# Second mixture of a three-stage kernel: work placed on the other side of skipped branches, and a 512-column product

## The chip, the cores and the metric

One core of a Trainium2 chip. The metric is device time in microseconds (us) of one execution of the whole kernel; smaller is better. A profile of one execution shows what each engine did: PE (TensorE; PEld is its weight load), DVE (VectorE), ACT (ScalarE), POOL (GpSimd) and SP (SyncE, which here only issues DMAs). Each engine has its own instruction stream and its own sequencer; they wait for one another with semaphores.

## The reference

Three stages, each fed by the one before. Only the last one matters for the change.

```python
attn = _attn_ref(x, a, B, C)              # linear attention, 4 x 8 heads x 768 steps
x = attn.transpose(0, 2, 1, 3).reshape(3072, 256)
x = _moe_ref(x, ...)                      # first mixture: 4 experts, every token through each
# second mixture: 8 experts, each token goes to one of them
expert_idx = argmax(x @ w_gate); gate_w = softmax(x @ w_gate)[expert_idx]
disp[e, k] = x[i]                         # k-th token of expert e, at most capacity = 768 of them
h = maximum(disp @ w1[e], 0)              # 256 -> 1024
y = h @ w2[e]                             # 1024 -> 256
out[i] = gate_w[i] * y[expert_idx[i], k]
```

## The kernel before

Every f32 operand of a product is split into a high and a low part (`h`, `l`), and a product is three matmuls: high by high, high by low, low by high.

The attention and the first mixture are one long stream without branches. The second mixture takes the experts 0 to 7 in turn. The tokens of an expert lie in a DRAM table `disp`; they are loaded in a block of up to 384 rows (`SLOTS`), transposed on PE (`turn`, L695) and split on ACT and DVE (`turned`, L703 and L704). How many tokens an expert has is known only when the kernel runs, so each expert has several programs, chosen by branches on the count: a narrow one for up to 256 tokens (`NARROW`), a wide one for up to 384, and a full one that does a wide block and then a second block of 384.

A block (`expert_block`, L737) loops over the 8 slices f of 128 hidden units. `up_part` (L715) makes a slice with six matmuls (L725 to L727) into a PSUM tile; ACT writes its high part after the ReLU (`ring_hh`, L729), DVE the low part (`ring_hl`, L730). Two slices later (`LAG` = 2) the slice is used for the second layer: for each group of 128 tokens, three matmuls of 256 columns, `hh` by `w2h`, `hh` by `w2l`, `hl` by `w2h` (L763 to L765), add into `yy`. At the block's end ACT scales each `yy` by the gate (`yo`, L773) and POOL scatters it to `out` by an indirect DMA (L774).

Between experts: `head(e)` (L732) does the first 256 columns of the first three slices (`HEAD`) of expert e before the count of e is asked, 18 matmuls in all; a wide or full program later adds the columns 256 to 384 of those three slices. Then come two branches in a row (L1090 and L1093): the narrow program, entered if the count is at most 256, and the wide or full ones, entered if it is more. Inside the latter, L1095 and L1097 choose between wide and full. Every branch runs on every engine. A program that isn't entered is jumped over, and on the other side stands, for each engine, an instruction that raises its semaphore by what the skipped program would have raised it (EVENT_SEMAPHORE in the trace), so that all later waits can count in program order. `hint` (L781) announces a later jump to PE's sequencer, and `align` (L784) sets the address of the next PE instruction to a slot of a block of 256 instructions. While an expert runs, its program also loads and splits the weights of the expert two further on (`split_w`, L365: a cast on ACT, a subtraction on DVE or POOL), and loads and turns the rows of the next one. The last expert has its own nesting of branches without jumps on its wide or full path.

Expert 0 is special: its first block is computed before the routing of the last tokens is done, on the rows known so far; `numbers["known"]` is their count. If that is below 384, the block has to be done once more; this is `redo_first` (L1061), asked at the very end (L1063).

Of the kernel before, what the change touches and what calls it, by code (L numbers as in the profile page):

```python
# [8 lines left out]
F32 = mybir.dt.float32  # L9
F32R = mybir.dt.float32r  # L10
# [21 lines left out]
SLOTS = 384  # L32
NARROW = 256
HEAD = 3
JOIN = 8
BLOCKS = [2, 3, 4, 4, 4, 4, 3]
MOST = max(BLOCKS)
NMAX = MOST * P
# [30 lines left out]
def attention_moe_moe_kernel(ctx: ExitStack, tc: tile.TileContext, aps: dict, cap: int):  # L69
# [282 lines left out]
    def weight_src(moe, e, c):  # L352
        w1, w2 = aps[f"w1_{moe}"][e], aps[f"w2_{moe}"][e]
        if c < 2:
            return w1[P * c:P * c + P, :]
        return w2[512 * (c - 2):512 * (c - 2) + 512, :].rearrange("(f p) d -> p f d", p=P)

    def load_w(moe, e, c):
        if (moe, e, c) not in given:
            pool, n = (late_pool[0], 2) if moe == 2 and (4 * e + c) % 5 > 2 else (sp, 3)  # L360
            given[moe, e, c] = pool.tile([P, FF], F32, tag="stage", name=f"stg{moe}_{e}_{c}", bufs=n)
        st = given[moe, e, c]
        nc.sync.dma_start(st if c < 2 else st.rearrange("p (f d) -> p f d", d=DM), weight_src(moe, e, c))

    def split_w(moe, e, c, lo):  # L365
        if (moe, e) not in W:
            W[moe, e] = [wp.tile([P, KD * FF], F32R, tag=n, name=f"{n}_{moe}_{e}") for n in ("w1h", "w1l", "w2h", "w2l")]
# [363 lines left out]

    def head(e):  # L732

        for f in range(HEAD):
            up_part(e, 0, f, 0, NARROW, f == HEAD - 1)

    def expert_block(e, k, n, extra, have=0, last=None, own=True):  # L737
        w2h, w2l = W[2, e][2:]
        g = gi[e, k]
        y = []  # L740
        at_ = 0

        def go():
            nonlocal at_
            at_ += 1
            for p in extra.get(at_, []):
                p()

        for f in range(NF + LAG):
            if f < NF:  # L750
                a = NARROW if f < have else 0
                if a < n:
                    up_part(e, k, f, a, n)
                go()
            js = [f - LAG] if LAG <= f < NF else list(range(NF - LAG, NF)) if f == NF else []
            for st in range(n // P):
                if js and js[0] == 0:
                    y.append(ps.tile([P, DM], F32, tag="acc", name=f"yy{e}_{k}_{st}", bufs=3))
                q = slice(P * st, P * st + P)
                for j in js:  # L760
                    hh, hl = ring[j % len(ring)]
                    c = slice(DM * j, DM * j + DM)
                    nc.tensor.matmul(y[st], lhsT=hh[:, q], rhs=w2h[:, c], start=j == 0, stop=False)  # L763
                    nc.tensor.matmul(y[st], lhsT=hh[:, q], rhs=w2l[:, c], start=False, stop=False)  # L764
                    nc.tensor.matmul(y[st], lhsT=hl[:, q], rhs=w2h[:, c], start=False, stop=j == NF - 1)  # L765
                if last and f == NF:
                    for p in last.get(st, []):
                        p()
            if js:
                go()  # L770
        for st in range(n // P):
            o = gp.tile([P, ROW], F32, tag="row", name=f"yo{e}_{k}_{st}", bufs=MOST)[:, :DM]
            nc.scalar.activation(o, y[st], AF.Copy, scale=g[:, st, 0:1])  # L773
            i = nc.gpsimd.indirect_dma_start(  # L774
                out=out[:, :],
                out_offset=bass.IndirectOffsetOnAxis(ap=g.bitcast(I32)[:, st, 1:2], axis=0),
                in_=o[:, :], in_offset=None, bounds_check=TOK - 1, oob_is_err=False)
            if own:
                disjoint("out", i)
# [7 lines left out]

    new_xT(0)
    steps0 = [attention_pieces(i, *xT[0], P * i) for i in range(2)]
    spare = wp.tile([P, 2 * FF], F32, tag="w2l", name="spare0")  # L790
    given[0, "bcq"] = given[1, "bcq"] = spare[:, 0:FF]
    given[1, "lt"] = spare[:, FF:].rearrange("p (h i) -> p h i", i=P)
    spare = wp.tile([P, 2 * FF], F32, tag="w2h", name="spare1")
# [9 lines left out]
    for tag, users in (("w1h", ((0, 2),)), ("w1l", ((1, 0), (3, 0))), ("w2h", ((1, 2), (3, 2))), ("w2l", ((2, 0),))):  # L803
        spare = wp.tile([P, 2 * FF], F32, tag=tag, name=f"early_{tag}")
        for e, c in users:
            given[1, e, c], given[1, e, c + 1] = spare[:, 0:FF], spare[:, FF:]

# [195 lines left out]
    W[2, 3] = [wp.tile([P, KD * FF], F32R, tag=n, name=f"{n}_2_3") for n in ("w1h", "w1l", "w2h", "w2l")]  # L1003
    for e in range(4, E2):
        W[2, e] = W[2, e - 4]
    for i in range(5, len(order)):
# [7 lines left out]

    make_ring()

    def first_block(e, n, two=False, over=None):
# [20 lines left out]
        expert_block(e, 0, n, extra, HEAD)  # L1038

    def second_into(e, tokens):  # L1040
        expert_block(e, 1, SLOTS, {})
        for k in range(2, nblk):
            with tc.If(tokens > SLOTS * k):
# [2 lines left out]
                turned(e, k)  # L1046
                expert_block(e, k, SLOTS, {})

    between = final_routing()
    between[10] = [load_counts]  # L1050
    first, second = ahead[0], ahead[1:]
    expert_block(0, 0, SLOTS, between, last={
        0: [lambda: ready(*first)], ST - 1: [lambda b=b: ready(*b) for b in second]})
    counts = numbers["all"]
    tokens = counts[0]
    if nblk > 1:
        with tc.If(tokens > SLOTS, preferred_fallthrough_block=True):
            second_into(0, tokens)
            align(JOIN)

    def redo_first():  # L1061

        with tc.If(numbers["known"] < SLOTS, preferred_fallthrough_block=True):  # L1063
            W[2, 0] = W[2, E2 - 1]
            for c in range(4):
                given[2, 0, c] = given[2, E2 - 1, c]
                load_w(2, 0, c)
                split_w(2, 0, c, nc.vector)
            load_rows(0, 0)
            ready(0, 0)  # L1070
            expert_block(0, 0, SLOTS, {}, own=False)

    for e in range(1, E2):
        tokens = counts[e]
        head(e)
        if e == E2 - 1:
            with tc.If(tokens > NARROW, preferred_fallthrough_block=True) as wide:
                if nblk > 1:
                    with tc.If(tokens > SLOTS, preferred_fallthrough_block=True) as more:
                        first_block(e, SLOTS, two=True)  # L1080
                        second_into(e, tokens)
                    with more.Else():
                        first_block(e, SLOTS)
                else:
                    first_block(e, SLOTS)
            with wide.Else():
                first_block(e, NARROW)
            redo_first()
            continue
        with tc.If(tokens <= NARROW, label=f"wide{e}", preferred_fallthrough_block=True):  # L1090
            hint(f"over{e}")
            first_block(e, NARROW)
        with tc.If(tokens > NARROW, label=f"over{e}", preferred_fallthrough_block=True):  # L1093
            if nblk > 1:
                with tc.If(tokens <= SLOTS, label=f"full{e}", preferred_fallthrough_block=True):  # L1095
                    first_block(e, SLOTS, over=f"next{e}")
                with tc.If(tokens > SLOTS, label=f"next{e}", preferred_fallthrough_block=True):  # L1097
                    first_block(e, SLOTS, two=True)
                    second_into(e, tokens)
                    align(JOIN)  # L1100
            else:
                first_block(e, SLOTS)


def prepare(inputs):
# [51 lines left out]
```

## Time and profile before

| | us |
|---|---|
| median of 3 runs (lowest, highest) | 791.07 (789.83, 792.62) |
| the profiled execution | 795.09 |
| its span, first to last instruction | 793.3 |
| busy PE / DVE / ACT / POOL | 766.5 / 440.8 / 282.9 / 189.0 |
| mean granted TensorE clock | 0.991 |

The span is what the trace's clock runs over; 1.8 us lie around it. A busy share counts the time in which an engine has an instruction in work; matmuls overlap, so on PE the distance between two starts (the pitch) says more than a duration.

In this data the trace shows expert 0 with a first and a second block (607.6 to 645.8 us), the experts 1 and 3 wide, 2, 4, 5 and 6 narrow, and 7 full (748.9 to 785.4 us). The count `known` is at least 384.

### The profile page before, as it was taken

The numbers are of one execution on the slowest core, as the hardware profiler recorded it, in microseconds if no ns is written. First come the engines' busy times: TensorE is split into PE (matmuls) and PEld (weight loads), VectorE is DVE, ScalarE is ACT, GpSimd is POOL, SyncE is SP. The second block draws the span as 40 slices with busy tenths as digits, with TensorE's granted clock in tenths as the row PEclk, the third lists the DMA queues.
The fourth block names the chain that finished last, engine by engine and source line by source line (L and its number), as shares of the span: only waits on it lengthen the run. The fifth ranks groups of instructions, "written<-read, shape, count | busy, mean of one in ns | idle before, by whom it ended". The sixth has DMA issues, their size and how long they took to land. (4 is left out here: it accounts for less than half of the span.)

```text
span 793.3 us, 13459 instructions
## 1 busy us (share of the span) xinstructions
PE 766.5 (97%) x5114; PEld 685.7 (86%) x5114; DVE 440.8 (56%) x884; ACT 282.9 (36%) x555; POOL 189.0 (24%) x227
## 2 busy tenths in 40 slices
PE   8999999999999999999999999999999989998996
PEld 7889999988878888888888888889999989897995
DVE  5886778457754577645666456543444323546321
ACT  2542543232323332233332323322453334555331
POOL 1010102212111122110221103011765313654211
PEclk9999999999999999999999999999999999999999
DMA  9753567523220232201322112040353214453100
GB/s 261 246 174 104 183 213 226 165 84 103 80 83 14 71 110 83 83 14 67 111 84 83 46 52 96 14 143 12 117 163 107 75 44 144 141 169 109 43 21 23
DMA packets 50195, 82.54 MB, mean 104 GB/s; under 512 B 5104, under 2 KB 35009, under 8 KB 50108
## 3 DMA queue, kind: packets, MB, share of 16 engines
q1 hardware_dynamic: 46340, 74.50, 30.0%
q0 software_dynamic: 2400, 6.11, 2.1%
q10 hardware_dynamic: 1368, 0.81, 0.4%
q8 instruction: 50, 0.82, 0.4%
q14 instruction: 37, 0.30, 0.1%
HBM read 65.56 MB, written 16.31 MB: 103 GB/s over the span
## 5 line engine op out<-in xcount | busy, mean ns | idle before, releaser
L502 DVE SCALAR_TENSOR_TENSOR hl<-ph,hh 128x512 fp32r<-128x512 f32 (+2 forms) x216 | 133.9, 620 | 221.7 <-ACT hh L501 218.1
L501 ACT ACTIVATE hh<-ph 128x512 fp32r<-128x512 f32 (+2 forms) x216 | 117.4, 543 | 348.4 <-PE ph L498 337.6
L496 PE MATMUL ph<-xh,w1h 128*128 128x512 f32 (+2 forms) x432 | 160.7, 372 | 1.6 <-DVE hl L502 1.6
L525 PE MATMUL acc<-hh,w2h 128*128 128x512 f32 (+2 forms) x432 | 158.1, 366 | 2.3 <-DVE x L541 1.4
L497 PE MATMUL ph<-xl,w1h 128*128 128x512 f32 (+2 forms) x432 | 156.4, 362 | 0.0
L498 PE MATMUL ph<-xh,w1l 128*128 128x512 f32 (+2 forms) x432 | 156.4, 362 | 0.0
L526 PE MATMUL acc<-hl,w2h 128*128 128x512 f32 (+2 forms) x432 | 156.3, 362 | 0.0
L527 PE MATMUL acc<-hh,w2l 128*128 128x512 f32 (+2 forms) x432 | 156.1, 361 | 0.0
L525 PEld LDWEIGHTS acc<-hh,w2h 128*128 128x128 f32 x432 | 81.2, 188 | 13.9 <-DVE x L541 2.2
L496 PEld LDWEIGHTS ph<-xh,w1h 128*128 128x128 f32 x432 | 81.3, 188 | 12.5 <-DVE hl L502 2.3
L730 DVE SCALAR_TENSOR_TENSOR ring_hl<-qh,ring_hh 128x384 fp32r<-128x384 f32 (+2 forms) x82 | 38.5, 472 | 95.8 <-ACT ring_hh L729 88.3
L498 PEld LDWEIGHTS ph<-xh,w1l 128*128 128x128 f32 x432 | 81.2, 188 | 10.5
L527 PEld LDWEIGHTS acc<-hh,w2l 128*128 128x128 f32 x432 | 81.3, 188 | 10.4
L526 PEld LDWEIGHTS acc<-hl,w2h 128*128 128x128 f32 x432 | 81.3, 188 | 9.4
L497 PEld LDWEIGHTS ph<-xl,w1h 128*128 128x128 f32 x432 | 81.3, 188 | 8.7
L549 POOL TENSOR_TENSOR x<-x,cmb 128x512 f32<-128x512 f32 (+2 forms) x40 | 48.5, 1234 | 153.0 <-DVE cmb L546 152.9
L729 ACT ACTIVATE ring_hh<-qh 128x384 fp32r<-128x384 f32 (+2 forms) x82 | 34.9, 425 | 83.8 <-PE qh L727 81.0
L765 PE MATMUL yy<-w2h,ring_hl 128*128 128x256 f32 x208 | 59.8, 287 | 0.0
L763 PE MATMUL yy<-w2h,ring_hh 128*128 128x256 f32 x208 | 59.7, 287 | 0.0
L764 PE MATMUL yy<-w2l,ring_hh 128*128 128x256 f32 x208 | 59.7, 287 | 0.0
L180 DVE TENSOR_TENSOR_SCAN lt<-abc,id 128x512 f32<-128x512 f32 x44 | 57.4, 1304 | 0.0
L725 PE MATMUL qh<-sxh,w1h 128*128 128x256 f32 (+2 forms) x132 | 42.0, 318 | 10.8 <-DVE ring_hl L730 3.0
(166 smaller groups left out, 1080.8 us busy)
## 6 DMA issues: line engine op xcount, KB each, us to landing
stg<-in_w SPq DMA_DIRECT2D x34, 512.0 KB
abc<-a_zero SPq DMA_DIRECT2D x21, 512.0 KB
bcr<-in_bc SPq DMA_DIRECT2D x19, 512.0 KB
disp<-zrow SPq DMA_DIRECT2D x12, 516.0 KB
nat<-in_nat SPq DMA_DIRECT2D x24, 256.0 KB
pb<-pT SPq DMA_DIRECT2D x16, 256.0 KB
rw<-disp SPq DMA_DIRECT2D x10, 387.0 KB
out<-zrow SPq DMA_DIRECT2D x6, 512.0 KB
```

Of the source, the lines that this page charges most:

```text
L180: nc.vector.tensor_tensor_scan(t["lt"][:, sl, :].rearrange("p h i -> p (h i)"), a_bc[:, sl, :].rearrange("p h i -> p (h i)"), id4.rearrang ...
L496: nc.tensor.matmul(ph[:, :n], lhsT=wh[:, c], rhs=xh[:, k, :n], start=k == 0, stop=False)
L497: nc.tensor.matmul(ph[:, :n], lhsT=wh[:, c], rhs=xl[:, k, :n], start=False, stop=False)
L498: nc.tensor.matmul(ph[:, :n], lhsT=wl[:, c], rhs=xh[:, k, :n], start=False, stop=k == KD - 1)
L501: nc.scalar.activation(hh[:, :n], ph[:, :n], AF.Relu)
L502: nc.vector.scalar_tensor_tensor(hl[:, :n], ph[:, :n], 0.0, hh[:, :n].bitcast(F32), ALU.max, ALU.subtract)
L525: nc.tensor.matmul(a[:, :n], lhsT=wh[:, c], rhs=hh[:, :n], start=f == 0, stop=False)
L526: nc.tensor.matmul(a[:, :n], lhsT=wh[:, c], rhs=hl[:, :n], start=False, stop=False)
L527: nc.tensor.matmul(a[:, :n], lhsT=wl[:, c], rhs=hh[:, :n], start=False, stop=f == NF - 1)
L763: nc.tensor.matmul(y[st], lhsT=hh[:, q], rhs=w2h[:, c], start=j == 0, stop=False)
L764: nc.tensor.matmul(y[st], lhsT=hh[:, q], rhs=w2l[:, c], start=False, stop=False)
L765: nc.tensor.matmul(y[st], lhsT=hl[:, q], rhs=w2h[:, c], start=False, stop=j == NF - 1)
```

## The change

The two halves of a second-layer weight become one tile `[128, 2, 2048]`, and the products of `hh` with both halves one matmul of 512 columns into a PSUM tile `[128, 2, 256]`; `hl` by `w2h` adds to its first half. At the block's end ACT scales the first half as before, and a new DVE instruction adds the second half times the gate. The three PSUM tiles are allocated once and used in rotation.

`head(e + 1)` no longer stands between the branches of two experts. It stands three times: in the Else of the branch that skips all wide programs, in the Else of the one that skips the full program, and at the end of the full program. In the Else of the narrow program stands `first_down`: the second-layer products of the first two slices for 256 tokens, which the wide and full programs then leave out. The repeat of expert 0's first block is asked right after expert 0, with `head(1)` in its Else. The last expert gets the same branches as the others. `JOIN` goes from slot 8 to 0, and expert 0's first block is aligned to slot 190 after its first slice.

```diff
-JOIN = 8
+JOIN = 0
+FIRST_BLOCK = 190
...
+    def weights(moe, e):
+        w1 = [wp.tile([P, KD * FF], F32R, tag=n, name=f"{n}_{moe}_{e}") for n in ("w1h", "w1l")]
+        w2 = wp.tile([P, 2, KD * FF], F32R, tag="w2", name=f"w2_{moe}_{e}")
+        return [*w1, w2[:, 0], w2[:, 1], w2]
...
+    def down_part(e, y, q, j):
+        w2 = W[2, e][4]
+        hh, hl = ring[j % len(ring)]
+        c = slice(DM * j, DM * j + DM)
+        nc.tensor.matmul(y, lhsT=hh[:, q], rhs=w2[:, :, c], start=j == 0, stop=False)
+        nc.tensor.matmul(y[:, 0], lhsT=hl[:, q], rhs=w2[:, 0, c], start=False, stop=j == NF - 1)
...
+    def sums(e, k, st):
...
+        return totals[(2 * e + k + st) % 3]
+
+    def first_down(e, y):
+
+        for j in range(LAG):
+            for st, t in enumerate(y):
+                down_part(e, t, slice(P * st, P * st + P), j)
...
-                    nc.tensor.matmul(y[st], lhsT=hh[:, q], rhs=w2h[:, c], start=j == 0, stop=False)
-                    nc.tensor.matmul(y[st], lhsT=hh[:, q], rhs=w2l[:, c], start=False, stop=False)
-                    nc.tensor.matmul(y[st], lhsT=hl[:, q], rhs=w2h[:, c], start=False, stop=j == NF - 1)
+                    if st >= len(early[1]) or j >= lead:
+                        down_part(e, y[st], q, j)
...
-            nc.scalar.activation(o, y[st], AF.Copy, scale=g[:, st, 0:1])
+            nc.scalar.activation(o, y[st][:, 0], AF.Copy, scale=g[:, st, 0:1])
+            nc.vector.scalar_tensor_tensor(o, y[st][:, 1], g[:, st, 0:1], o, ALU.mult, ALU.add)
...
+    def choose(cond, label, yes, no):
+        with tc.If(cond, label=label, preferred_fallthrough_block=True) as choice:
+            yes()
+        if no:
+            with choice.Else():
+                no()
+
+    def full_program(e, tokens, y):
+        first_block(e, SLOTS, y, LAG, two=True)
+        second_into(e, tokens)
+        head(e + 1)
+        if e + 1 < E2:
+            align(JOIN)
+
+    def wide_programs(e, tokens, y, after):
...
+        choose(tokens <= SLOTS, f"full{e}", lambda: first_block(e, SLOTS, y, LAG, over=f"next{e}"), None)
+        choose(tokens > SLOTS, f"next{e}", lambda: full_program(e, tokens, y), after)
+
+    def narrow_program(e, y):
+        hint(f"over{e}")
+        first_block(e, NARROW, y, 0)
+
+    def first_once_more():
+        load_rows(0, 0)
+        ready(0, 0)
+        expert_block(0, 0, SLOTS, {}, own=False)
+        head(1)
+        align(JOIN)
+
     between = final_routing()
+    between[1] = [lambda: align(FIRST_BLOCK)]
...
-        with tc.If(tokens > SLOTS, preferred_fallthrough_block=True):
-            second_into(0, tokens)
-            align(JOIN)
+        with tc.If(counts[0] > SLOTS, preferred_fallthrough_block=True):
+            hint("again")
+            second_into(0, counts[0])
+    choose(numbers["known"] < SLOTS, "again", first_once_more, lambda: head(1))
     for e in range(1, E2):
         tokens = counts[e]
-        head(e)
...
+        after = (lambda: head(e + 1)) if e + 1 < E2 else None
+        y = [sums(e, 0, st) for st in range(NARROW // P)]
+        choose(tokens <= NARROW, f"wide{e}", lambda: narrow_program(e, y), lambda: first_down(e, y))
+        choose(tokens > NARROW, f"over{e}", lambda: wide_programs(e, tokens, y, after), after)
```

## Rows read from the trace of the kernel before

**Rows 1.** The page: busy time of each engine, and PE's granted clock in 40 slices.
```profile
PE 766.5 (97%) x5114; PEld 685.7 (86%) x5114; DVE 440.8 (56%) x884; ACT 282.9 (36%) x555; POOL 189.0 (24%) x227
PEclk9999999999999999999999999999999999999999
```
**Rows 2.** Two windows: us, busy PE, PEld, DVE, ACT, POOL, granted clock, DMA, GB/s.
```profile
652.90:656.40 3.50, 3.50 (x16) 3.50 (x16) 0.29 (x1) 1.21 (x2) 1.98 (x1) 0.52 0.00 0
717.80:721.30 3.50, 3.19 (x16) 2.89 (x14) 0.42 (x1) 0.89 (x3) 0.75 (x1) 0.51 0.42 143
```
**Rows 3.** Timeline of PE, starts of heads: start, us, instruction, idle before and releaser.
```profile
669.89 0.38 PE L725 MATMUL qh<-sxh,w1h 128*128 128x256 f32 x1 [0.75 <-ACTq L1097]
...
682.40 0.28 PE L765 MATMUL yy<-w2h,ring_hl 128*128 128x256 f32 x1
683.37 0.38 PE L725 MATMUL qh<-sxh,w1h 128*128 128x256 f32 x1 [0.69 <-ACTq L1093]
...
748.86 0.39 PE L725 MATMUL qh<-sxh,w1h 128*128 128x256 f32 x1 [0.68 <-ACTq L1093]
```
**Rows 4.** Line L1093's branch around 682 us: min/median/max ns, first and last start.
```profile
L1093 PEldq COMPARE_BRANCH  x1: 343/343/343, 681.7 to 681.7; - x1
...
L1093 PEldq EVENT_SEMAPHORE  x1: 51/51/51, 682.7 to 682.7; - x1
...
L1093 ACTq EVENT_SEMAPHORE  x1: 17/17/17, 683.3 to 683.3; - x1
```
**Rows 5.** Timeline of PE: after expert 0, and after a skipped narrow program.
```profile
645.55 0.28 PE L765 MATMUL yy<-w2h,ring_hl 128*128 128x256 f32 x1
647.25 0.36 PE L725 MATMUL qh<-sxh,w1h 128*128 128x256 f32 x1 [1.42 <-ACT yo L773]
...
649.36 0.28 PE L727 MATMUL qs<-sxh,w1l 128*128 128x256 f32 x1
650.63 0.33 PE L725 MATMUL qh<-sxh,w1h 128*128 128x128 f32 x1 [0.99 <-DVEq L1090]
```
**Rows 6.** Timeline of PE: ends of a 256-column run (27 matmuls) and a 512-column run (66).
```profile
764.59 0.28 PE L763 MATMUL yy<-w2h,ring_hh 128*128 128x256 f32 x1
...
767.70 0.28 PE L765 MATMUL yy<-w2h,ring_hl 128*128 128x256 f32 x1
...
471.42 0.50 PE L496 MATMUL ph<-xh,w1h 128*128 128x512 f32 x1
...
486.29 0.39 PE L498 MATMUL ph<-xh,w1l 128*128 128x512 f32 x1
```
**Rows 7.** Groups of instructions by shape: line, count, busy us, mean ns, idle before.
```profile
L763 PE MATMUL yy<-w2h,ring_hh 128*128 128x256 f32 x208 | 59.7, 287 | 0.0
L773 ACT ACTIVATE yo<-yy,gi 128x256 f32<-128x256 f32 x26 | 12.2, 477 | 15.4 <-PE yy L765 15.4
L730 DVE SCALAR_TENSOR_TENSOR ring_hl<-qh,ring_hh 128x256 fp32r<-128x256 f32 x34 | 14.2, 422 | 40.2 <-ACT ring_hh L729 34.6 <-issue 5.5
```
**Rows 8.** Timelines inside narrow expert 4: PE's two waits, and DVE before the second.
```profile
712.92 0.39 PE L725 MATMUL qh<-sxh,w1h 128*128 128x256 f32 x1 [0.39 <-DVE ring_hl L730]
...
716.54 0.39 PE L725 MATMUL qh<-sxh,w1h 128*128 128x256 f32 x1 [1.93 <-DVE ring_hl L730]
...
712.79 3.36 DVE L372 TENSOR_TENSOR w2l<-stg,w2h 128x1024 fp32r<-128x1024 f32 x1
```
**Rows 9.** Line L1090's branch around 650 us, columns as in rows 4.
```profile
L1090 DVEq COMPARE_BRANCH  x1: 69/69/69, 650.1 to 650.1; - x1
L1090 DVEq EVENT_SEMAPHORE  x1: 21/21/21, 650.6 to 650.6; - x1
```
**Rows 10.** Branch rows of lines L1090 and L1063, whole run.
```profile
L1090 PEldq COMPARE_BRANCH  x10: 72/190/232, 647.4 to 747.0; - x10
...
L1063 PEldq COMPARE_BRANCH  x1: 3018/3018/3018, 783.9 to 783.9; - x1
...
L1063 POOLq INC_SWDGE_SEM  x1: 530/530/530, 790.4 to 790.4; - x1
```

More of the change, by code (lines that the diff above doesn't have):

```diff
@@ L363, in load_w @@
         nc.sync.dma_start(st if c < 2 else st.rearrange("p (f d) -> p f d", d=DM), weight_src(moe, e, c))
+    def weights(moe, e):
+        w1 = [wp.tile([P, KD * FF], F32R, tag=n, name=f"{n}_{moe}_{e}") for n in ("w1h", "w1l")]
+        w2 = wp.tile([P, 2, KD * FF], F32R, tag="w2", name=f"w2_{moe}_{e}")
+        return [*w1, w2[:, 0], w2[:, 1], w2]
     def split_w(moe, e, c, lo):
         if (moe, e) not in W:
-            W[moe, e] = [wp.tile([P, KD * FF], F32R, tag=n, name=f"{n}_{moe}_{e}") for n in ("w1h", "w1l", "w2h", "w2l")]
+            W[moe, e] = weights(moe, e)
         h, l = W[moe, e][2 * (c // 2):2 * (c // 2) + 2]
@@ L732, in head, with expert_block @@
     def head(e):
-        for f in range(HEAD):
+        for f in range(HEAD if e < E2 else 0):
             up_part(e, 0, f, 0, NARROW, f == HEAD - 1)
-    def expert_block(e, k, n, extra, have=0, last=None, own=True):
-        w2h, w2l = W[2, e][2:]
+    def down_part(e, y, q, j):
[4 more added lines that the diff above has]
+        nc.tensor.matmul(y[:, 0], lhsT=hl[:, q], rhs=w2[:, 0, c], start=False, stop=j == NF - 1)
+    totals = []
+    def sums(e, k, st):
+        if not totals:
+            totals.extend(ps.tile([P, 2, DM], F32, tag="acc", name=f"yy{i}", bufs=3) for i in range(3))
+        return totals[(2 * e + k + st) % 3]
[3 more added lines that the diff above has]
+                down_part(e, t, slice(P * st, P * st + P), j)
+    def expert_block(e, k, n, extra, have=0, last=None, own=True, early=(0, ())):
         g = gi[e, k]
-        y = []
+        lead, y = early[0], list(early[1])
         at_ = 0
@@ L756, in expert_block @@
             for st in range(n // P):
-                if js and js[0] == 0:
-                    y.append(ps.tile([P, DM], F32, tag="acc", name=f"yy{e}_{k}_{st}", bufs=3))
+                if js and st == len(y):
+                    y.append(sums(e, k, st))
                 q = slice(P * st, P * st + P)
                 for j in js:
-                    hh, hl = ring[j % len(ring)]
-                    c = slice(DM * j, DM * j + DM)
-                    nc.tensor.matmul(y[st], lhsT=hh[:, q], rhs=w2h[:, c], start=j == 0, stop=False)
-                    nc.tensor.matmul(y[st], lhsT=hh[:, q], rhs=w2l[:, c], start=False, stop=False)
-                    nc.tensor.matmul(y[st], lhsT=hl[:, q], rhs=w2h[:, c], start=False, stop=j == NF - 1)
+                    if st >= len(early[1]) or j >= lead:
+                        down_part(e, y[st], q, j)
                 if last and f == NF:
@@ L789, in attention_moe_moe_kernel @@
     steps0 = [attention_pieces(i, *xT[0], P * i) for i in range(2)]
-    spare = wp.tile([P, 2 * FF], F32, tag="w2l", name="spare0")
+    both = wp.tile([P, 2, 2 * FF], F32, tag="w2", name="spare0")
+    spare = both[:, 1]
     given[0, "bcq"] = given[1, "bcq"] = spare[:, 0:FF]
     given[1, "lt"] = spare[:, FF:].rearrange("p (h i) -> p h i", i=P)
-    spare = wp.tile([P, 2 * FF], F32, tag="w2h", name="spare1")
+    spare = both[:, 0]
     given[1, "m0"] = spare[:, 0:512].rearrange("p (h i) -> p h i", i=P)
@@ L802, in attention_moe_moe_kernel @@
     given[1, 2, 2], given[1, 2, 3] = spare[:, 0:FF], spare[:, FF:]
-    for tag, users in (("w1h", ((0, 2),)), ("w1l", ((1, 0), (3, 0))), ("w2h", ((1, 2), (3, 2))), ("w2l", ((2, 0),))):
-        spare = wp.tile([P, 2 * FF], F32, tag=tag, name=f"early_{tag}")
+    both = wp.tile([P, 2, 2 * FF], F32, tag="w2", name="early_w2")
+    for spare, users in (
+            (wp.tile([P, 2 * FF], F32, tag="w1h", name="early_w1h"), ((0, 2),)),
+            (wp.tile([P, 2 * FF], F32, tag="w1l", name="early_w1l"), ((1, 0), (3, 0))),
+            (both[:, 0], ((1, 2), (3, 2))), (both[:, 1], ((2, 0),))):
         for e, c in users:
@@ L1000, in load_counts @@
         numbers["all"] = nc.values_load_multi_w_load_instructions(cnt[1][0:1, 0:E2], min_val=0, max_val=TOK)[1]
-    W[2, 3] = [wp.tile([P, KD * FF], F32R, tag=n, name=f"{n}_2_3") for n in ("w1h", "w1l", "w2h", "w2l")]
+    W[2, 3] = weights(2, 3)
     for e in range(4, E2):
@@ L1015, in attention_moe_moe_kernel, with first_block @@
     make_ring()
-    def first_block(e, n, two=False, over=None):
+    def first_block(e, n, y, lead, two=False, over=None):
         extra = {}
@@ L1037, in first_block @@
                 add(m + 3, lambda w=order[i + 5]: load_w(2, *w))
[L1038 removed]
+        expert_block(e, 0, n, extra, HEAD, early=(lead, y))
     def second_into(e, tokens):
@@ L1047, in second_into @@
                 expert_block(e, k, SLOTS, {})
+    def choose(cond, label, yes, no):
[11 more added lines that the diff above has]
+    def wide_programs(e, tokens, y, after):
+        if nblk == 1:
+            first_block(e, SLOTS, y, LAG)
+            head(e + 1)
+            return
+        choose(tokens <= SLOTS, f"full{e}", lambda: first_block(e, SLOTS, y, LAG, over=f"next{e}"), None)
[9 more added lines that the diff above has]
+        align(JOIN)
     between = final_routing()
+    between[1] = [lambda: align(FIRST_BLOCK)]
     between[10] = [load_counts]
@@ L1054, in attention_moe_moe_kernel @@
     counts = numbers["all"]
-    tokens = counts[0]
     if nblk > 1:
-        with tc.If(tokens > SLOTS, preferred_fallthrough_block=True):
-            second_into(0, tokens)
-            align(JOIN)
[L1061 to L1071, printed above, removed]
+        with tc.If(counts[0] > SLOTS, preferred_fallthrough_block=True):
+            hint("again")
+            second_into(0, counts[0])
@@ L1073, in attention_moe_moe_kernel @@
+    choose(numbers["known"] < SLOTS, "again", first_once_more, lambda: head(1))
     for e in range(1, E2):
         tokens = counts[e]
-        head(e)
[L1076 to L1102, printed above, removed]
+        after = (lambda: head(e + 1)) if e + 1 < E2 else None
```

## The prediction

> **What bounds the kernel now.** The page comes first: PE is in work for 97% of the span, no other engine for more than 56% [rows 1]. So time is won only where PE has less to do, waits less, or runs at a higher clock. [...] Then the timeline of PE, read for starts: within the second mixture PE pauses almost only between programs. Before each head but the first it has idled 0.68 to 0.75 us, six times, and the releaser is a branch instruction of ACT [rows 3]. The branch's own rows tell why: PE has jumped at 681.7 + 0.34 us, its own count is raised at 682.7, when its last matmul is through, but ACT, still scaling the block, reaches its raising instruction only at 683.3 [rows 4]; the head starts 0.07 us later. After a skipped narrow program PE has idled 0.99 us for DVE in the same way, and after expert 0 it has idled 1.42 us [rows 5].
>
> **The change part by part.** All sums are made against the profiled execution, 795.09 us (span 793.3 and 1.8 around it), and the difference is then taken from the median, 791.07.
>
> *The 512-column product.* A run of 27 matmuls of 256 columns has 26 pitches in 767.70 - 764.59 = 3.11 us, 119.6 ns each; 66 of 512 columns have 65 in 14.87 us, 228.8 ns [rows 6]. Two of 256 become one of 512: 2 x 119.6 - 228.8 = 10.4 ns. There are 208 such pairs [rows 7], all on PE's path: -2.2 us (bounds 2.0 and 2.3 from the last digits of the starts).
> [...]
>
> *Heads in the Else.* There the semaphores need no raising before the head: its own first instructions can carry the difference, and what it reads (the turned rows, free PSUM tiles) was finished inside the program just left. From the last start before a head to its first the pitch is 683.37 - 682.40 = 0.97 us instead of 0.12 [rows 3], so 0.85 is lost, and the first matmul after a pause costs some 0.1 more: 6 x 0.95 = 5.7 us. Not all goes: PE now makes one more jump (over `first_down`), and its sequencer is only 0.7 us ahead of its matmuls (it jumps at 681.7, the last matmul starts at 682.4). I leave 0.25 us each: -4.2 us. Bounds: 0.6 left each, -2.1; nothing left, -5.7.
>
> *`first_down` on the other side of the narrow program.* Experts 1 and 3 pause 650.63 - 649.36 - 0.12 = 1.15 us, for DVE to pass the skip [rows 5]; the two are alike. `first_down` is 4 x (228.8 + 119.6) ns = 1.39 us of products that are only moved, and covers that. With 0.1 for the first matmul and 0.2 left each: -2.1 us (bounds -1.0 and -2.5).
>
> *After expert 0.* 647.25 - 645.55 - 0.12 = 1.58 us [rows 5]. ACT's `yo` is named, but the program's waits there are for older instructions; what is executed is an aligned jump without a hint. Afterwards it is a hinted jump into the Else: 0.3 left, -1.3 us (bounds +0.3 and -1.6).
>
> *The clock.* A stretch of 3.5 us at 0.52 loses 1.7 us, and there are two [rows 2]. Before the first, PE idled 1.42 and 0.99 us, the pauses just removed; before the second 0.39 and 1.93 us inside narrow expert 4, where DVE is held by a weight subtraction of 3.36 us [rows 8], which stays. I let the first go and the second stay: -1.6 us (bounds 0 and -3.3).
>
> *Expert 7.* It had no skip on its way; now it has two, past its narrow program (covered by `first_down`) and past its wide one. What no row shows is a skip right behind another. DVE needs 0.5 us from branch to raising [rows 9], so PE would wait some 0.5 us. The jump itself has two prices: unhinted ones over a narrow program (84 matmuls) took PE up to 0.23 us, the one over `redo_first` (126 matmuls) 3.02 us [rows 10]. The wide program of expert 7 has 88 left, nearer to 84: +0.5 us in all, bounds 0 and +3.0.
>
> *DVE's new instruction.* 26 more (one per `yo` [rows 7]) of about 0.42 us, the price of `ring_hl` with 256 columns [rows 7]: 10.9 us on an engine in work for 56%. They lie between a block's end and the next head's `ring_hl`, which needs 0.7 us of PE and an ACT pass first; the cover is that head. But ACT comes late there too: it passes the branch only 0.9 us after PE's last start [rows 3, 4] and then has a second jump, so the first `ring_hl` ends some 2.4 us after that start, about when the next product wants it. And in narrow experts 2, 4 and 5 PE waits for DVE later on anyway (expert 4: [rows 8]), so part of a head's gain is lost again there. +0.5 us, bounds 0 and +2.5.
>
> *Small things.* The align after the first slice of expert 0 is one jump in a long straight stream: +0.2, bounds 0 and +1.4 (the pause after expert 0). The tail loses the branch of `redo_first`, whose raising on POOL takes 0.53 us behind the last scatter [rows 10], and wins DVE's 0.42 us before the first of three scatters: 0, bounds -1.5 and +0.5. The weight tile and its cuts in the first two stages hold the same data at the same times: 0, because nothing there changes its order.
>
> Sum: -2.2 - 4.2 - 2.1 - 1.3 - 1.6 + 0.5 + 0.5 + 0.2 = -10.2 us. That is 784.9 for the profiled execution, and 791.07 - 10.2 = 780.9, say **781 us**.
>
> **The rivals.**
>
> *The waits come back behind the head.* PE starts a head 0.95 us earlier, but ACT and DVE, which must scale, add and jump first, don't; then PE waits at the first second-layer product instead, and DVE's stalls in narrow experts grow. For it: DVE's waits [rows 8], and ACT as the last releaser before heads [rows 3]. Against it: the head is 18 x 0.12 = 2.2 us, and the product after it wants only what was made from the head's first third. Then of 4.2 us a quarter stays and the clock may still drop: -2.2 - 1.0 - 2.1 - 1.3 - 0.8, and the losses 0.5 for expert 7, 1.0 for DVE and 0.2, make -5.7, **785.4 us**.
>
> *Jumps that miss.* The new form has more unhinted jumps of PE on its way: four over `first_down`, three to it, two over the other copy of the head, one past expert 7's wide program, ten in all. Each that costs 3.02 us as at L1063 [rows 10], less the 0.7 us by which the sequencer is ahead, adds 2.3 us. From five misses on (11.5 us) the gain of 10.2 is gone; at eight the time is 781 + 8 x 2.3 = **799 us**, slower than before. For it: the pause after expert 0 (1.42 us idle behind an unhinted jump) looks like such a miss. Against it: all ten targets are near, and ten jumps at L1090 took 72 to 232 ns.
> [...]
>
> *Both sides cancel.* One or two misses, a clock stretch more (+1.7) and the first rival together leave -5.7 + 4.6 + 1.7, about nothing: **791 us**.
>
> **How the numbers follow.** Forecast (777 to 784) 0.60; waits come back 0.23; cancel 0.08; jumps that miss 0.09. The edges of the forecast's own range come from the head term's bounds and the clock's. The range that should hold 8 in 10 is 776 to 788: down by the bounds of heads and clock (-1.5 and -1.7, with some of the rest), up to the first rival and one miss. This kernel's runs can tell 0.3%, 2.4 us, from no change; so faster means below 788.7. Faster 0.83, same 0.08, slower 0.09.
>
> **What would show it.** In the profile after: 208 matmuls of 512 columns with a pitch near 229 ns; the idle time before each head under 0.3 us with no branch of ACT as releaser; no idle for a branch of DVE before the 128-column matmuls of experts 1 and 3; the window near 653 us at full clock; and PE's branch rows all under 0.4 us on the path. [...]

## The result, and the profile after

The changed kernel takes **777.31 us** in the median (4 runs, 775.79 to 780.77), the kernel before 790.7 in the same comparison (789.83 to 792.62): ratio 0.984, 95% interval 0.9813 to 0.9867. The profiled execution takes 778.5 us, its span is 776.7. The forecast was 781, range 776 to 788.

The page, where [rows 1] stood before:
```profile
PE 762.0 (98%) x4906; PEld 673.4 (87%) x4906; DVE 450.2 (58%) x910; ACT 283.4 (36%) x555; POOL 187.5 (24%) x227
PEclk9999999999999999999999999999999999999999
```
PE has 208 matmuls fewer than before, and DVE 26 instructions more. The two windows of [rows 2], over other work now, at the full clock:
```profile
652.90:656.40 3.50, 3.50 (x22) 3.37 (x22) 1.14 (x4) 2.95 (x5) 1.87 (x1) 1.00 0.24 85
717.80:721.30 3.50, 3.50 (x24) 3.21 (x23) 1.82 (x4) 1.81 (x5) 3.50 (x3) 1.00 0.01 2
```
The timeline of PE around the head of expert 3, where the kernel before idled 0.69 us ahead of the head [rows 3] and 0.99 us behind a skipped narrow program [rows 5, the same place in expert 1]: the last product of expert 2, the head's first; its last and `first_down`'s first; `first_down`'s last and the first of the wide program.
```profile
678.10 0.28 PE L748 MATMUL yy<-w,ring_hl 128*128 128x256 f32 x1
678.21 0.28 PE L731 MATMUL qh<-sxh,w1h 128*128 128x256 f32 x1
...
680.25 0.28 PE L733 MATMUL qs<-sxh,w1l 128*128 128x256 f32 x1
680.38 0.45 PE L747 MATMUL yy<-w,ring_hh 128*128 128x512 f32 x1
...
681.71 0.28 PE L748 MATMUL yy<-w,ring_hl 128*128 128x256 f32 x1
681.82 0.22 PE L731 MATMUL qh<-sxh,w1h 128*128 128x128 f32 x1
```
No idle is left at any of the three joints, and the same holds at every head (only expert 7's wide program still starts late, by 0.5 us). PE's branch rows (line, queue, count, min/median/max ns) take at most 0.44 us, so none of its jumps was late. The groups by shape show the new product and DVE's addition, 0.48 us where I had put 0.42:
```profile
L1077 PEldq COMPARE_BRANCH  x30: 72/192/441, 645.7 to 768.3; - x30
```
```profile
L747 PE MATMUL yy<-w,ring_hh 128*128 128x512 f32 x208 | 76.2, 398 | 0.0
L748 PE MATMUL yy<-w,ring_hl 128*128 128x256 f32 x208 | 58.3, 280 | 0.0
```
```profile
L796 DVE SCALAR_TENSOR_TENSOR yo<-yy,gi,yo 128x256 f32<-128x256 f32 x26 | 12.4, 483 | 13.1 <-ACT yo L795 12.8
```

**One trace of before was not enough.** The sum was made against an execution of 795.09 us. A second trace of the same kernel is of one of 786.89, the fastest of its ten; so neither trace is of an ordinary execution:

> The kernel before, unchanged, for a second trace of it. The first trace is of an execution of 795.09 us, 4 us above the median. Theory E (an ordinary execution has no collision of DVE with POOL in narrow experts 4 and 5, or fewer, and one clock stretch less): the profiled execution takes 789 to 792 us, its heads wait 0.85 us each and its skips 1.15 us as in the first trace, but the pitches of PE inside experts 2, 4 and 5 lose under 2 us in place of 4.1. Rival (the collisions are always there, and the 4 us lie before the second mixture): the second mixture takes 171 to 172 us from the first counts to the last product again.

Median 791.23 us (10 runs, 786.89 to 792.6), ratio to itself 1.0007 (0.9982 to 1.0032). Its second mixture, from its first product to the start of its last, runs from 606.23 to 777.49 us, 171.3, against 177.6 in the first trace. By the rival's measure, from the first counts (612.14 us here, 613.52 there), it takes 165.4 against 171.6, and not 171 to 172 again. So theory E holds, though the execution was faster still than it said. Heads and skips wait as before (678.88 to 679.85 is again 0.97 us from start to start):
```profile
678.88 0.28 PE L765 MATMUL yy<-w2h,ring_hl 128*128 128x256 f32 x1
679.85 0.38 PE L725 MATMUL qh<-sxh,w1h 128*128 128x256 f32 x1 [0.69 <-ACTq L1093]
```
But the waits inside the narrow experts, 4.1 us in the first trace, are 0.9 here, and both clock stretches of [rows 2] are missing. So some 6 us come and go from execution to execution of one program; the experiments below show what most of them are.

The table sets the forecast's terms beside the traces, in us. For each kind of pause in the second mixture it adds up by how much PE's pitches in the kernel before are longer than their columns take, and subtracts what the kernel after still has of that kind:

| term | forecast | from the first trace | from the second |
|---|---|---|---|
| 512 columns | -2.2 | -2.2 | -2.2 |
| six heads | -4.2 | -5.3 | -5.1 |
| `first_down`, two skips | -2.1 | -2.3 | -2.3 |
| after expert 0 | -1.3 | -1.6 | -1.3 |
| clock stretches | -1.6 | -3.3 | 0 |
| waits in narrow experts (DVE) | +0.5 | -3.4 | -0.2 |
| expert 7's skips | +0.5 | +0.5 | +0.5 |
| expert 0's second block (align) | +0.2 | +0.2 | +0.2 |
| sum | -10.2 | -17.4 | -10.4 |
| second mixture, start to last product start | | -16.9 | -10.6 |
| behind it (the tail) | 0 | -1.4 | -0.9 |
| ahead of it | 0 | +1.7 | +3.1 |
| whole span | | -16.6 | -8.4 |

The second mixture begins at 606.2 to 609.3 us in these three traces. I count that as spread: over all the traces of this document it begins at 606.2 to 608.8 us in the old form and at 606.1 to 609.5 in the new.

### The profile page after: what moved, and what is told of

The parts are those of the page before. It is cut to its first block, busy times and chain, and to the rows that moved or that the text cites. A ratio compares the mean times of both kernels' runs of the same rounds, so it can differ in the third digit from the quotient of the medians.

```text
span 776.7 us, 13173 instructions
## 1 busy us (share of the span) xinstructions
PE 762.0 (98%) x4906; PEld 673.4 (87%) x4906; DVE 450.2 (58%) x910; ACT 283.4 (36%) x555; POOL 187.5 (24%) x227
## 5 line engine op out<-in xcount | busy, mean ns | idle before, releaser
L502 PE MATMUL ph<-xh,w1h 128*128 128x512 f32 (+2 forms) x432 | 160.7, 372 | 1.6 <-DVE hl L508 1.6
L531 PE MATMUL acc<-hh,w 128*128 128x512 f32 (+2 forms) x432 | 158.1, 366 | 2.3 <-DVE x L547 1.4
L532 PE MATMUL acc<-hl,w 128*128 128x512 f32 (+2 forms) x432 | 156.3, 362 | 0.0
L533 PE MATMUL acc<-hh,w 128*128 128x512 f32 (+2 forms) x432 | 156.1, 361 | 0.0
L531 PEld LDWEIGHTS acc<-hh,w 128*128 128x128 f32 x432 | 81.2, 188 | 13.9 <-DVE x L547 2.2
L502 PEld LDWEIGHTS ph<-xh,w1h 128*128 128x128 f32 x432 | 81.3, 188 | 12.5 <-DVE hl L508 2.2
L533 PEld LDWEIGHTS acc<-hh,w 128*128 128x128 f32 x432 | 81.3, 188 | 10.4
L532 PEld LDWEIGHTS acc<-hl,w 128*128 128x128 f32 x432 | 81.3, 188 | 9.3
L747 PE MATMUL yy<-w,ring_hh 128*128 128x512 f32 x208 | 76.2, 398 | 0.0
L748 PE MATMUL yy<-w,ring_hl 128*128 128x256 f32 x208 | 58.3, 280 | 0.0
L747 PEld LDWEIGHTS yy<-w,ring_hh 128*128 128x128 f32 x208 | 39.1, 188 | 6.1
```

What stands on the lines that cost most here:

```text
L502: nc.tensor.matmul(ph[:, :n], lhsT=wh[:, c], rhs=xh[:, k, :n], start=k == 0, stop=False)
L531: nc.tensor.matmul(a[:, :n], lhsT=wh[:, c], rhs=hh[:, :n], start=f == 0, stop=False)
L532: nc.tensor.matmul(a[:, :n], lhsT=wh[:, c], rhs=hl[:, :n], start=False, stop=False)
L533: nc.tensor.matmul(a[:, :n], lhsT=wl[:, c], rhs=hh[:, :n], start=False, stop=f == NF - 1)
L747: nc.tensor.matmul(y, lhsT=hh[:, q], rhs=w2[:, :, c], start=j == 0, stop=False)
L748: nc.tensor.matmul(y[:, 0], lhsT=hl[:, q], rhs=w2[:, 0, c], start=False, stop=j == NF - 1)
```

## The experiments

The kernel before has a median of 790.4 to 791.9 us in the comparisons of this table, so differences between medians of two rows are good to some 1.5 us; the ratios are each to the kernel before of the same comparison.

| kernel | median us (runs) | ratio to before, 95% |
|---|---|---|
| after, three 256-column products | 796.38 (7) | 1.0074 (1.0048 to 1.0101) |
| after, no `first_down` | 788.91 (12) | 0.9973 (0.9951 to 0.9994) |
| after, no hints | 806.5 (5) | 1.0213 (1.0185 to 1.024) |
| after, repeat asked at the end | 777.46 (5) | 0.9839 (0.9814 to 0.9863) |
| after, `JOIN` 30 | 802.04 (6) | 1.0131 (1.01 to 1.0163) |
| after, `JOIN` 78 | 789.79 (12) | 0.998 (0.996 to 1.0001) |
| three 256-column products, `JOIN` 217 | 786.34 (6) | 0.9929 (0.9901 to 0.9957) |
| before, 512-column product alone | 794.6 (12) | 1.0021 (1.0002 to 1.004) |
| before, all subtractions on DVE | 789.95 (12) | 0.999 (0.9969 to 1.001) |
| after, `JOIN` 78, all on DVE | 780.18 (6) | 0.9878 (0.9853 to 0.9903) |
| after, all on DVE | 777.53 (5) | 0.9842 (0.9814 to 0.987) |

**Undo the product.**
```diff
-        nc.tensor.matmul(y, lhsT=hh[:, q], rhs=w2[:, :, c], start=j == 0, stop=False)
+        nc.tensor.matmul(y[:, 0], lhsT=hh[:, q], rhs=w2[:, 0, c], start=j == 0, stop=False)
+        nc.tensor.matmul(y[:, 0], lhsT=hh[:, q], rhs=w2[:, 1, c], start=False, stop=False)
...
-            nc.vector.scalar_tensor_tensor(o, y[st][:, 1], g[:, st, 0:1], o, ALU.mult, ALU.add)
```


> The kernel after with the second layer's high half as two products of 256 columns again (three in all per slice, no addition by DVE); heads and first_down as after. My theory: 208 pairs x 10.4 ns, +2.2 us over the kernel after, all of it in the pitch of PE. [...] Second rival, DVE's addition costs as much as the columns give: 0 or less than 0.

It is 19 us slower than the kernel after, which no theory had. The pitches of the products explain 2.2 of it. Most of the rest stands in PE's timeline, behind the narrow experts 2, 4, 5 and 6; here the first of the four:
```profile
678.70 0.28 PE L749 MATMUL yy<-w,ring_hl 128*128 128x256 f32 x1
682.19 0.36 PE L731 MATMUL qh<-sxh,w1h 128*128 128x256 f32 x1 [3.22 <-issue]
```
The branches of PE in that stretch (676 to 683 us) and the window behind the second late head, columns as in [rows 2]:
```profile
L1077 PEldq COMPARE_BRANCH  x3: 238/314/3886, 677.8 to 682.3; - x3
```
```profile
718.00:722.00 4.00, 3.91 (x18) 3.94 (x19) 0.85 (x2) 0.77 (x2) 0.00 (x0) 0.50 0.78 210
```
"Issue" means that PE waited for no semaphore: its sequencer sat 3.9 us in one jump, a hinted one, to the head. Four idles of 3.2, 3.0, 2.5 and 2.5 us make 11.3 us, and behind three of them, not behind the third, the granted clock was 0.50 for 13.7 us in all. The windows behind the third and the fourth:
```profile
735.60:739.00 3.40, 3.40 (x29) 3.40 (x30) 1.27 (x3) 1.15 (x3) 0.00 (x0) 1.00 0.06 16
751.20:754.60 3.40, 3.40 (x18) 3.40 (x17) 1.00 (x3) 1.16 (x3) 0.00 (x0) 0.50 0.44 117
```

**Undo `first_down`.** The narrow program loses its Else, and the wide ones make all second-layer products themselves.
```diff
-        choose(tokens <= NARROW, f"wide{e}", lambda: narrow_program(e, y), lambda: first_down(e, y))
+        choose(tokens <= NARROW, f"wide{e}", lambda: narrow_program(e, y), None)
...
```


> The kernel after without the Else side of the narrow program (no first_down): a wide program makes all its second-layer products itself. My theory: PE waits again for DVE to pass the skip, 1.15 us each before experts 1 and 3, and some 1 us at expert 7, which now has a skip too: +2.3 to +3.4 us over the kernel after, with idle of about 1 us before the first matmul behind each of these three skips. Rival: PE is ahead only because DVE is, and the wait comes back with first_down too: 0 to +0.5.

The three waits came, 0.99, 1.08 and 1.76 us of idle (experts 1, 3, 7); the first:
```profile
646.80 0.28 PE L733 MATMUL qs<-sxh,w1l 128*128 128x256 f32 x1
648.07 0.33 PE L731 MATMUL qh<-sxh,w1h 128*128 128x128 f32 x1 [0.99 <-DVEq L1077]
```
But the kernel lost 11.6 us between medians, 5.7 between the two profiled executions. In this trace the second mixture is 8.2 us longer than in the kernel after: the three skips make 3.8 of it, a stretch at a granted clock of 0.50 behind expert 3's wait 1.7, and in experts 2, 4 and 5 PE also waited 0.8 us each for a DVE that was held by one long subtraction, three times 3.1 us. The trace is of one of the fastest of the 12 executions (784.17 of 784.01 to 790.92), so what the median lost beyond it isn't shown. DVE and then POOL in expert 2:
```profile
671.40 3.09 DVE L378 TENSOR_TENSOR w<-stg,w 128x1024 fp32r<-128x1024 f32 x1
```
```profile
670.29 3.12 POOL L378 TENSOR_TENSOR w1l<-stg,w1h 128x1024 fp32r<-128x1024 f32 x1 [1.87 <-DMA out<-yo,gi]
```

**Take the hints away.** `hint` does nothing.

> The kernel after without any of its branch hints. Theory A (jumps that miss): the six jumps over programs that had a hint miss as the one at the end did, 3.0 us less the 0.7 us by which the sequencer is ahead: about 2.3 us each, +14 to +16 us, and the branch rows of PE show some 3 us. Theory B (targets are loaded anyway): under +1 us, branch rows under 0.45 us.

It is 29 us slower than the kernel after. Seven heads start late, and a jump takes up to 5.4 us; the group of their first matmuls and PE's branches:
```profile
L731 PE MATMUL qh<-sxh,w1h 128*128 128x256 f32 (+2 forms) x132 | 42.0, 318 | 20.1 <-issue 15.7 <-DVE yo L796 3.9 <-PEq L1077 0.3
```
```profile
L1077 PEldq COMPARE_BRANCH  x30: 72/182/5443, 643.6 to 792.3; - x30
```
Theory A holds, with seven late jumps in place of six and larger ones than I had priced: 20.1 us of idle, and 13.7 us at a granted clock of 0.50. The far jumps of the new form depend on their hints: with them none took more than 0.44 us.

**The repeat of expert 0 asked at the end.** `head(1)` follows expert 0 directly; the test and its program go behind expert 7, as in the kernel before.

> The kernel after with the test for a second pass of expert 0 at the end again, as before; head 1 follows expert 0's test directly. Theory A: the shorter tail of the kernel after (6.7 us from PE's last start to the end against 8.15 before) comes from that test's move: +1.4 us in the tail, and within 0.5 us nothing elsewhere. Theory B: the tail is set by the last scatter and its landing: tail within 0.3 us of the kernel after.

No change, and the tail, from PE's last start to the end, is 6.7 us again (769.21 to 775.9). So theory A is out. The traces show where the tail got shorter, from 8.15 and 7.6 us: in the first trace of before POOL's raising behind this test [rows 10] begins 5.2 us after PE's last start, and a drain of 1.55 us follows it; here it begins after 2.3 us, and POOL's drain runs while the last scatter lands (in the kernel after 3.71 us, from 772.0 us on). Why it begins earlier stays open.

**Only the addresses.** `align` counts the positions of PE's instructions in multiples of 256, the number in its call; in the counts below an instruction takes one position and a matmul two, itself and its weight load (the page of the kernel after has 4906 of each). Where the parts of a narrow expert then lie, counted from the programs and not read from a trace, and how many of the four heads behind narrow experts are late in the trace:

| kernel | narrow program with its hint | the two tests behind it | late heads |
|---|---|---|---|
| after, `JOIN` 0 | 78 to 218 | 237, 238, same block | 0 |
| three products, `JOIN` 0 | 78 to 248 | 19, 20, next block | 4 |
| after, `JOIN` 30 | 108 to 248 | 11, 12, next block | 4 |
| after, `JOIN` 78 | 156 to 40, over the border | 59, 60, next block | 0 |
| three products, `JOIN` 217 | 39 to 209 | 236, 237, same block | 0 |

> The kernel after, JOIN 30 in place of 0: the same instructions in the same order, only the place of PE's programs against the multiples of 256 positions that align counts in moves by 30. A matmul takes two positions (its weights and itself). In the kernel after, a narrow program with its hint and the two tests behind it lies at 78 to 238, in one block of 256; here the tests lie at 11 and 12 of the next block, some 20 positions behind the border, as in the kernel with three 256-column products (19 and 20). Theory A (a hinted jump misses if a border lies between its hint and its test): the heads after experts 2, 4, 5 and 6 start some 3 us late each, as there; +11 to +17 us over the kernel after (788 to 794 us). Theory B (the misses came from the longer product, or its missing addition on DVE): within 1 us of the kernel after.

> The kernel after, JOIN 78: the tests behind a narrow program lie at 59 and 60 of the next block, with about 40 positions (20 products, some 3 us) of the narrow program behind the border; the wide programs' tests stay in the block of their hint or one border on, as in the kernel after. Theory A: four misses as with JOIN 30, +11 to +17 us. Theory C (what the hint asked for is fetched only once the border is crossed, and needs some 3 us): the 40 positions cover most of it, under 1 us per jump, +0 to +4 us. Theory B: within 1 us of the kernel after.

> The kernel with three 256-column products (heads and first_down as after), JOIN 217 in place of 0: the head's copy starts a block, and a narrow program, now 30 positions longer, with its hint and its tests lies at 39 to 237 of one block. Theory A: the four misses go, and what is left is the products' own price: +2.2 us over the kernel after (778 to 781 us). Theory B (three products cost 19 us by themselves): 794 to 798 us. [...]

`JOIN` 30 has the instructions of the kernel after, in their order, and is 24.7 us slower. All four heads are late (3.56, 1.79, 2.47 and 2.43 us of idle):
```profile
679.81 0.28 PE L748 MATMUL yy<-w,ring_hl 128*128 128x256 f32 x1
683.64 0.55 PE L731 MATMUL qh<-sxh,w1h 128*128 128x256 f32 x1 [3.56 <-issue]
```
The late heads are not the whole price, though. The second mixture is 25.5 us longer here than in the kernel after (186.1 against 160.7): late heads make 10.9, four stretches of 3.4 us at a granted clock of 0.50 cost nearly 7, and some 8 are waits for DVE in the narrow experts 2, 4 and 5, of the kind shown further down; the longest in expert 2:
```profile
677.00 0.39 PE L731 MATMUL qh<-sxh,w1h 128*128 128x256 f32 x1 [1.97 <-DVE ring_hl L736]
```
Theory A's four late heads came, and theory B is out: neither the third product nor the missing addition made the jumps late. Three products at `JOIN` 217 have no late head (pitch 0.12 us) and win 10 us back. Their 778 to 781 us did not come, though: the profiled execution took 783.07, the median is 786.34. What is left beside the products' 2.2 us are three idles of 0.2 to 0.6 us for nothing but the sequencer (two of them behind jumps of 2.3 and 2.6 us) and, again, up to 2.1 us at a time for DVE in the narrow experts 4 and 5.

`JOIN` 78 refutes theory A as I had put it: a border does lie between hint and test, and no head is late. It is late elsewhere. The jump that comes right after the head, to a `first_down` that now lies beyond the next border, takes PE's sequencer 3.6 and 3.2 us and costs 1.5 us of idle in expert 3 and 1.1 in expert 7 (in expert 1 it takes 1.9 us and costs nothing); head and `first_down` of expert 3:
```profile
681.05 0.28 PE L748 MATMUL yy<-w,ring_hl 128*128 128x256 f32 x1
681.17 0.28 PE L731 MATMUL qh<-sxh,w1h 128*128 128x256 f32 x1
...
683.21 0.28 PE L733 MATMUL qs<-sxh,w1l 128*128 128x256 f32 x1
685.01 0.47 PE L747 MATMUL yy<-w,ring_hh 128*128 128x512 f32 x1 [1.52 <-issue]
```
Theory C's jump price holds at the heads, its time (+0 to +4) does not: it came to +12.5, of which the waits for DVE below make some 7 us, these two jumps 2.9 and a clock stretch 1.8. Shown is that a change of addresses alone decides which jumps are late: at `JOIN` 0 none took over 0.44 us, at 30 the four to the heads up to 4.19, at 78 the three to `first_down` 1.9 to 3.6. In the two kernels with four late heads the border is crossed by the jump over `first_down`, a dozen or a score of positions ahead of the test; at `JOIN` 78 the narrow program runs across it some 40 positions before its end. Which of the two matters, the way or the distance, is not settled.

**The product alone.** Of the change, only the weight tile, the 512-column matmul and DVE's addition, in the kernel before.

> The kernel before with the 512-column product and DVE's addition alone; heads, skips and the end of the program as before. Theory A: -2.2 us against the kernel before (208 pairs x 10.4 ns), less what DVE's 26 additions give back in the narrow experts, where PE waits for DVE: -2.2 to 0. Rival: the product is most of the whole gain of 13.4 us, as its removal cost 19 us: -10 us or more.

Not faster: +0.2%. Where the head follows the branches, DVE's addition delays DVE's jump, and with it the head; the wait before head 2, which was 0.75 us in [rows 3]:
```profile
665.88 0.28 PE L747 MATMUL yy<-w,ring_hl 128*128 128x256 f32 x1
667.40 0.35 PE L730 MATMUL qh<-sxh,w1h 128*128 128x256 f32 x1 [1.24 <-DVEq L1116]
```
The six pitches before heads sum to 9.0 us over the columns' time, against 5.3: +3.8. The pause after expert 0 [rows 5] is gone, -1.6, and the columns give -2.2: together 0. In the kernel after the heads do not wait for DVE (their pitch is 0.11 us), and there the addition costs PE nothing.

**DVE against POOL.** Wherever these traces have a DVE subtraction of over 3 us, one of POOL had begun ahead of it. With `JOIN` 78 they start 0.1 us apart; DVE and POOL in expert 2:
```profile
674.48 3.37 DVE L378 TENSOR_TENSOR w<-stg,w 128x1024 fp32r<-128x1024 f32 x1
```
```profile
674.38 2.38 POOL L378 TENSOR_TENSOR w<-stg,w 128x1024 fp32r<-128x1024 f32 x1
```
POOL ends at 676.76, DVE at 677.85, 1.1 us later, about what its subtraction takes alone (1.2). In all the traces, where two such subtractions overlap, one ends about its own time after the other has ended (in six of them DVE 1.08 to 1.21 us after POOL, POOL 2.25 to 2.38 us after DVE), and it is the one that started later wherever the starts are more than 0.01 us apart. So all four go to DVE, in three kernels:
```diff
-            add(m, lambda w=order[i], lo=(nc.vector if c in (1, 2) else nc.gpsimd): split_w(2, *w, lo))
+            add(m, lambda w=order[i], lo=nc.vector: split_w(2, *w, lo))
```


> The kernel before with all four weight subtractions of an expert on DVE (two of them were on POOL). Theory D (a subtraction of DVE that overlaps one of POOL waits for it: 3.36 and 3.09 us in place of 1.2): no DVE subtraction takes more than 1.3 us, the waits of PE inside the narrow experts 4 and 5 (0.39 and 1.93, 0.9 us) go, and with them the clock stretch at 718 us: -3 to -5 us against the kernel before. Rival (DVE is simply full in a narrow block): two more subtractions of 1.23 us make its waits longer, by up to 2.4 us in each of four narrow experts: +2 to +10 us.

> The kernel after with JOIN 78, and all four weight subtractions on DVE. With JOIN 78 alone PE waits 3.3 and 4.0 us for DVE in experts 2 and 4, and a stretch behind the second runs at the lower clock. Theory D: these 7.3 us and some 1.8 us of clock go: 779 to 783 us against 789.8. Rival (DVE is full): no change or slower, 788 to 798 us.

> The kernel after with all four weight subtractions on DVE. In it no DVE subtraction waits for POOL's by the luck of its timing, so theory D gives nothing: within 1.5 us of the kernel after (776 to 779 us). Rival (DVE is full): +1 to +6 us.

With `JOIN` 78 it wins 9.6 us (789.79 to 780.18), as theory D said (7.3 and 1.8); the waits for DVE and the clock stretch are gone from the trace, and the two late jumps, still there, cost 1.2 us less. In the kernel after it changes nothing, also as said, but not for the reason that the expectation gives: four of DVE's subtractions did wait behind POOL there (1.89 to 2.44 us), while PE lost only 0.3 and 0.4 us to DVE. In the closest pairs DVE started first and POOL waited, which costs PE nothing. DVE and then POOL in expert 4 of the kernel after:
```profile
704.87 1.21 DVE L378 TENSOR_TENSOR w<-stg,w 128x1024 fp32r<-128x1024 f32 x1
```
```profile
705.05 3.30 POOL L378 TENSOR_TENSOR w<-stg,w 128x1024 fp32r<-128x1024 f32 x1 [0.39 <-ACT w L377]
```
In the kernel before, the groups of DVE show all twenty subtractions at their own price, and the narrow experts' waits and the second clock stretch are gone from the trace; its first clock stretch, after the pauses of [rows 5], is still there:
```profile
L372 DVE TENSOR_TENSOR w1l<-stg,w1h 128x1024 fp32r<-128x1024 f32 x10 | 12.3, 1225 | 3.6 <-ACT w1h L371 3.6
L372 DVE TENSOR_TENSOR w2l<-stg,w2h 128x1024 fp32r<-128x1024 f32 x10 | 12.2, 1218 | 1.5 <-ACT w2h L371 1.5
```
The median there moves by 0.7 us, inside its uncertainty; -3 to -5 was expected. The second trace of before suggests a reason: an execution can have few collisions to lose. How many of the ordinary ones do is not shown.

No version beats the changed kernel: two tie with it.

## Why the prediction was right

**The sum.** -10.2 was forecast from the first trace, -16.6 came against it, -13.4 between medians, -8.4 against the second trace. Right were the mechanisms of the product, the heads, `first_down` and expert 7, and in part that of the pause after expert 0. A part of the fit is luck. The clock stretches and DVE's waits, which I took for steady terms, differ from execution to execution of one kernel. Against the first trace both came out larger than forecast, by 5.6 us together. Against the second the terms sum to -10.4 only because errors cancel: the 1.6 us of clock were not there to win, and heads, `first_down` and DVE's waits gave 1.8 us more.

**512 columns.** A pair of products takes 0.348 us in the kernel after (eight pairs from 662.76 to 665.54 us), as [rows 6] gave (228.8 + 119.6 ns). The size was right, its standing alone was not: without the heads' move it is worth nothing, and it shortens a narrow program by some 30 positions and `first_down` by 8, without which the new form doesn't fit its block at `JOIN` 0.

**Heads.** Mis-sized: -4.2 was forecast with 0.25 us left each, and nothing is left (pitch 0.11 us). The sequencer's lead covers two short jumps: ahead of expert 3's head they begin at 677.2 us, 0.9 us before the last matmul starts, and take 0.20 and 0.34 us.

**`first_down`.** -2.1 forecast, -2.3 measured. Its removal shows 1.0 to 1.8 us of idle per skip; without it expert 7 waits 1.76 us, more than the 1 us of my expectation.

**After expert 0.** The size was right (-1.3 against -1.3 to -1.6), the reason only in part. It was a late jump, as the rival suspected, and the first trace of before has its row (L785 is the `align`), which I had not read:
```profile
L785 PEldq COMPARE_BRANCH  x1: 3011/3011/3011, 643.8 to 643.8; - x1
```
With the product alone the pause was gone too, with the same unhinted form; the row of the same jump there:
```profile
L800 PEldq COMPARE_BRANCH  x1: 322/322/322, 642.8 to 642.8; - x1
```
So this jump is late or not without any change of its form. What differs is the number of instructions ahead of it, and so its address; that the address decides here too is inferred from the address runs, not shown by a run of its own.

**The clock, and DVE's new instruction.** Here a step failed, though the total came out. I wrote that in narrow expert 4 DVE is held by a weight subtraction of 3.36 us, "which stays", and that PE's waits for DVE in the narrow experts 2, 4 and 5 would grow. The trace in front of me had the answer: that subtraction took 3.36 us [rows 8], others of its group 1.2, and POOL's had begun 0.1 us ahead of it (712.70 against 712.79):
```profile
712.70 2.37 POOL L372 TENSOR_TENSOR w2l<-stg,w2h 128x1024 fp32r<-128x1024 f32 x1
```
The wait was a collision, a matter of who starts first. In the kernel after DVE starts first at this place, PE's waits shrink to 0.3 us in expert 2 and 0.4 in expert 4, and the second clock stretch is gone. That the first stretch would go with the pauses of [rows 5] was no safe term either: the second trace has pauses of 1.18 and 0.99 us there and no stretch.

**Expert 7.** +0.5 forecast, +0.5 measured: a pitch of 0.60 us in place of 0.12 at 737.04 us.

**The rivals.** Waits that come back behind the head: none. Both sides cancel: no. Jumps that miss: none in this kernel, but its last hinted test lies 18 positions before a border, and the same instructions 30 positions on are 24.7 us slower. A chance of 0.09 fitted the two prices that I had read; the 3.01 us of L785 was a third, of a jump on PE's way, and positions could have been counted from the program.

## What to carry to other kernels

Count where a hinted jump, its hint and its target lie against the blocks that the alignment counts, and repeat the count after every edit that changes the number of instructions: here a change of addresses alone cost 24.7 us, with the collisions and clock stretches that came with it, more than the whole edit won. Before taking a wait for a property of a kernel, trace it a second time, and compare each long instruction with the fastest of its group. An added instruction at the end of a block is not free where something behind a branch waits for its engine to pass: with the product alone the pitches before the six heads grew by 3.8 us.

## What the runs showed of the hardware

- The late jumps took PE's sequencer 1.9 us (`JOIN` 78) to 5.4 us (no hints), with a hint (up to 4.2, `JOIN` 30) or without; all others in the second mixture 0.07 to 0.45 us, except one of 0.61 without hints.
- Where a subtraction of DVE and one of POOL, 128 x 1024, met, one ended 1.08 to 1.21 us (DVE) or 2.25 to 2.38 us (POOL) after the other, about the time that it took alone (1.2 and 2.4 us); it lasted up to 3.38 us on DVE (`JOIN` 78) and 3.38 on POOL (no `first_down`).
- PE's granted clock fell to 0.50 for some 3.5 us or more behind some pauses and not behind others as long: with three products an idle of 2.53 us before 735.57 us did not lower it and one of 2.49 before 750.45 did. In the first trace of before pauses of 1.4 and 1.0 us did [rows 2, 5], in the second 1.2 and 1.0 us at the same places did not. What decides is open.
